# Attention then a mixture of experts on one core: the first sequence's queries taken in two passes, and the running expert begun in the 11th slot

## The chip, the cores and the metric

The kernel runs on one core of one Trainium2 chip, as one launch. The metric is the time of that launch on the device in microseconds (us), the median of 3 runs. Less is better. The core has a matmul engine (TensorE, PE in the rows; PEld is its weight load, which overlaps), a vector engine (VectorE, DVE), a scalar engine (ScalarE, ACT), a general engine (GpSimd, POOL) and a queue engine (SyncE, SP) that here issues nearly all transfers between the chip's memory and the core. Each engine runs its own instructions strictly in the order of the program and waits for others through semaphores.

## What is computed

Causal attention over 4 sequences of 576 tokens with 8 heads of 64, whose scores get a bias from a running sum; then 8 experts, all of them applied to all 2304 tokens, weighted by a normalised gate.

```python
cum = np.cumsum(np.maximum(s, 0.0), axis=-1)
bias = -(cum[:, :, :, None] - cum[:, :, None, :])
scores = np.where(causal, -1e9, q @ k.T / sqrt(D) + np.minimum(bias, 0.0))
attn = softmax(scores)
x = (attn @ v) laid out as [2304, 512]
P = exp(x @ w_gate - max); 8 rounds of row and column normalisation
out = sum over e of P[:, e] * (relu(x @ w1[e]) @ w2[e])
```

All of it is in 32-bit floats. The kernel carries each operand of a matmul as a high part and a low part (what is left after the rounding to the matmul's format), and makes three products of them.

## The kernel before

**The attention** works on head pairs: `g` counts the 16 pairs (4 sequences of 4 pairs). A pair has 5 slots, one for each block of queries `i`: four of 128 queries, and a last one that takes the 64 left of both heads together. Slot `i` needs the first `i + 1` blocks of keys. `slots` (line 662) is the list of all 80, pair after pair. The loop over `ti` (line 711) writes a pipeline: `st0` makes the scores of slot `ti` (line 497, tile `sc`), the row minimum on VectorE (line 506) and the exponential on ScalarE (line 538); `st1` the division, one slot later; `st2` the transposes (line 569, tile `tr`), two slots later; `st3` the product with v (line 599, tile `pv`), for blocks 0 and 1 together and for blocks 2, 3 and 4 together, three slots after the last of them. Its result goes into the tile `xh`, the operand of the experts.

**What a head needs** is made by `load_head` (line 329; four transfers, two halves of q and two of k, each copied to both halves of the partitions) and `prep_head` (line 408): q in two forms (`qa`, `qb`), k in two forms (`ka`, `kb`), made by GpSimd and VectorE, with two or three short transfers of bias rows and one of `qa` into `qb`, all issued from SP. `qa` and `qb` are four fixed tiles each, used by head number modulo 4 (names qa_224, qb_225 to qa_236, qb_237 in the order of before; qa_218, qb_219 to qa_230, qb_231 in that of the changed kernel). `prep_head` stands after slots 1 and 3 of the pair before.

**The running expert** is expert 0, computed beside the attention in four units of 256 hidden columns. A visit is one unit applied to the 256 to 384 tokens of one or two blocks (`EARLY`): `g1_half` (line 148) makes 6 of the 12 matmuls of a hidden block, `g2_chunk` (line 177) 6 matmuls of 512 columns. `Stream` (line 200) keeps them in a queue; `fill` (line 685) takes from it so that the queue is empty when the next sequence ends. A sequence's four visits are put into the queue in its last slots (`ti` 22, 42, 62); the fourth sequence's run after the attention. Each unit's weights come by two transfers of 512 KB (`w_load_early`, line 654, tile `wraw`) and four splits into high and low parts (lines 110 and 111, tile `w`). Two units fit; the first two are loaded and split from `ti` 4 on.

**The rest**, experts 1 to 7, runs after the attention in one long stretch of matmuls (lines 1012, 1133, 1190).

**What sets the order.** The scheduler that writes the engines' orders follows the priorities of the program and its own clock; the result is a fixed order on each engine. On SP each transfer carries one of eight semaphores in turn and waits for the transfer eight before it.

## Time and profile before

| | us |
|---|---|
| median of 3 runs | 1697.48 (1696.84 to 1698.23) |
| the profiled execution | 1700.61 |
| its span in the profile | 1698.7 |
| TensorE busy | 1667.0 (98%) |
| VectorE busy | 1192.2 (70%) |
| GpSimd busy | 871.9 (51%) |
| ScalarE busy | 838.5 (49%) |

The span runs from the first to the last instruction that the profile saw. Busy time of an engine is the time in which at least one of its instructions ran. A TensorE that is busy may run at half its clock: the granted clock, PEclk, is 1.00 at 2.4 GHz, and a mean of 0.75 over a stretch says that it spent half of it at 1.2 GHz. A line such as "L497" is a line of the kernel before; "x48" is a count of instructions.

### The profile page before, as it was taken

How to read it: one execution, taken by the hardware profiler on the slowest of the kernel's cores; microseconds unless marked ns; L12 is line 12 of the kernel's file. 1: busy time of each engine (PE TensorE's matmuls, PEld its weight loads, DVE VectorE, ACT ScalarE, POOL GpSimd, SP SyncE). 2: the span in 40 equal slices, each digit the busy share in tenths (PEclk: the TensorE clock that was granted, in tenths of full speed). 3: DMA queues.
4: the chain of work that ended last, by engine and by line, in shares of the span. 5: the costliest groups of instructions: out<-in, count | busy, mean ns of one | idle time of the engine just before them, and what ended most of it. 6: DMA issues, size and time to landing. Idle time of an engine off the chain costs nothing.

```text
span 1698.7 us, 31233 instructions
## 1 busy us (share of the span) xinstructions
PE 1667.0 (98%) x11149; PEld 1569.4 (92%) x11149; DVE 1192.2 (70%) x2309; ACT 838.5 (49%) x1820; POOL 871.9 (51%) x799
## 2 busy tenths in 40 slices
PE   7899999999999999999999999999999999999999
PEld 6788888889899999998889999999999999999999
DVE  6757666655767766776448777777777777777777
ACT  5976666633543444444235444444444544444443
POOL 6757857622654554554314455554544555554453
PEclk8989999999999999999999999999999999999999
DMA  7767666374777767865965656666697666666562
GB/s 195 222 186 215 201 195 188 98 284 156 269 260 240 262 213 232 261 226 194 338 195 175 198 176 198 189 187 189 187 316 235 210 190 188 188 186 187 176 197 88
DMA packets 204988, 352.11 MB, mean 207 GB/s; under 512 B 21089, under 2 KB 103009, under 8 KB 204801
## 3 DMA queue, kind: packets, MB, share of 16 engines
q1 hardware_dynamic: 204352, 349.19, 64.6%
q8 instruction: 89, 1.46, 0.4%
q10 hardware_dynamic: 480, 0.92, 0.2%
q14 instruction: 67, 0.54, 0.1%
HBM read 249.94 MB, written 94.81 MB: 203 GB/s over the span
## 4 chain that ended last, share of the span: by engine, by line
PE 85%; DVE 7%; DMA 2%; ACT 2%; issue 2%; POOL 1%; SPq 1%; ACTq 0%; DVEq 0%; POOLq 0%
PE c L1012 31%; PE zz L1133 13%; PE zz L1190 11%; PE y L1190 10%; PE g L148 4%; PE g L177 4%; PE sc L497 3%; DVE s L987 3%; PE pv L599 3%; PE tr L569 2%; PE c L177 1%; PE c L148 1%; DVE h L252 1%; DVE z L255 1%; DMA rawk<-kT 1%
## 5 line engine op out<-in xcount | busy, mean ns | idle before, releaser
L252 POOL TENSOR_TENSOR w2o<-r,w2o 128x512 fp32r<-128x512 f32 x189 | 274.0, 1470 | 320.9 <-ACT w2o L1170 313.3
L1012 PE MATMUL c<-xS,w1o 128*128 128x384 f32 x1344 | 270.2, 337 | 4.4 <-DVE z L255 2.8
L1190 PE MATMUL zz<-w2o,h 128*128 128x256 f32 x2016 | 273.1, 279 | 0.0
L1190 PEld LDWEIGHTS zz<-w2o,h 128*128 128x128 f32 x2016 | 263.8, 188 | 0.1
L1133 PE MATMUL zz<-w2p,h 128*128 128x512 f32 x1008 | 254.7, 391 | 0.4 <-ACT h L975 0.4
L975 ACT ACTIVATE h<-z 128x384 fp32r<-128x384 f32 x252 | 130.3, 525 | 226.6 <-DVE z L255 224.7
L976 DVE SCALAR_TENSOR_TENSOR h<-z,h 128x384 fp32r<-128x384 f32 x252 | 193.3, 775 | 65.5 <-ACT h L975 61.8
L1012 PEld LDWEIGHTS c<-xS,w1o 128*128 128x128 f32 x1344 | 226.7, 188 | 8.7 <-DVE z L255 6.9
L987 DVE SCALAR_TENSOR_TENSOR s<-z,s 128x384 f32<-128x384 f32 x224 | 189.9, 885 | 60.0 <-ACT s L1050 58.7
L1133 PEld LDWEIGHTS zz<-w2p,h 128*128 128x128 f32 x1008 | 187.1, 188 | 30.3 <-ACT h L975 0.7
L252 POOL TENSOR_TENSOR h<-s,h 128x384 fp32r<-128x384 f32 x112 | 137.7, 1236 | 128.8 <-ACT h L983 127.7
L1012 PE MATMUL c<-x,w1o 128*128 128x384 f32 x1008 | 202.1, 335 | 0.2 <-DVE z L255 0.2
L1190 PE MATMUL y<-w2o,h 128*128 128x256 f32 x1512 | 199.7, 279 | 0.0
L1190 PEld LDWEIGHTS y<-w2o,h 128*128 128x128 f32 x1512 | 193.7, 188 | 0.0
L255 DVE TENSOR_TENSOR z<-c,t 128x384 f32<-128x384 f32 x252 | 136.3, 550 | 58.1 <-PE c L1012 53.2
L1012 PEld LDWEIGHTS c<-x,w1o 128*128 128x128 f32 x1008 | 169.5, 188 | 0.4 <-DVE z L255 0.4
L1116 DVE SCALAR_TENSOR_TENSOR a<-zz,prob,a 128x256 f32<-128x256 f32 (+1 forms) x210 | 111.0, 530 | 80.9 <-PE zz L1190 50.8
L983 ACT CAST h<-s 128x384 fp32r<-128x384 f32 x224 | 112.1, 514 | 87.0 <-DVE s L987 85.8
L1012 PE MATMUL c<-xS,wp 128*128 128x384 f32 x672 | 134.5, 336 | 1.4 <-DVE z L255 1.4
L1012 PEld LDWEIGHTS c<-xS,wp 128*128 128x128 f32 x672 | 118.9, 188 | 9.6 <-DVE z L255 2.7
L1170 ACT CAST w2o<-r 128x1024 fp32r<-128x1024 f32 x98 | 102.4, 1046 | 47.8 <-PE y L1190 37.9
L252 POOL TENSOR_TENSOR wp<-s,wp 128x512 fp32r<-128x512 f32 x56 | 79.5, 1420 | 83.7 <-ACT wp L911 72.5
(149 smaller groups left out, 2738.2 us busy)
## 6 DMA issues: line engine op xcount, KB each, us to landing
w1o<-w1d SPq DMA_DIRECT2D x392, 256.0 KB
w1d<-wp SPq DMA_DIRECT2D x84, 512.0 KB
r<-wu SPq DMA_DIRECT2D x70, 512.0 KB
r<-w2d SPq DMA_DIRECT2D x56, 512.0 KB
sa<-wu SPq DMA_DIRECT2D x28, 512.0 KB
w2d<-sb SPq DMA_DIRECT2D x56, 256.0 KB
wraw<-wu SPq DMA_DIRECT2D x22, 512.0 KB
xS<-xd_S SPq DMA_DIRECT2D x12, 768.0 KB
```

The costliest lines, as they stand in the source:

```text
L148: nc.tensor.matmul(ps[:, :n], lhsT=w1[:, w, o : o + P], rhs=xcols(b, x, k, n0, n), start=(k == 0 and t == 0), stop=(k == KD - 1 and t == 2),)
L252: (eng or nc.gpsimd).tensor_tensor(out=out, in0=a, in1=b, op=ALU.subtract)
L255: (eng or nc.gpsimd).tensor_tensor(out=out, in0=a, in1=b, op=ALU.add)
L975: mark["a"] = nc.scalar.activation(t[:, 0], z, AF.Relu)
L976: mark["v"] = nc.vector.scalar_tensor_tensor(out=t[:, 1], in0=z, scalar=0.0, in1=t[:, 0].bitcast(F32), op0=ALU.max, op1=ALU.subtract,)
L983: nc.scalar.copy(t[:, 0], z)
L987: nc.vector.scalar_tensor_tensor(out=out, in0=z, scalar=0.0, in1=other, op0=ALU.max, op1=op)
L1012: mm = nc.tensor.matmul(ps, lhsT=w[:, wl, k], rhs=x[:, xl, k], start=(fresh and k == 0 and t == 0), stop=(k == 1 and t == 2), skip_group_c ...
L1116: nc.vector.scalar_tensor_tensor(out=a, in0=ps, scalar=prob[:, c, e : e + 1], in1=a, op0=ALU.mult, op1=ALU.add)
L1133: mm = nc.tensor.matmul(zb[ci], lhsT=h[:, a, ci * P : (ci + 1) * P], rhs=w[:, b_], start=(ui == 0 and f == 0 and t == 0), stop=(ui == UPE ...
L1170: nc.scalar.copy(w[:, :, 0], r)
L1190: nc.tensor.matmul(ps, lhsT=h[:, a, ci * P : (ci + 1) * P], rhs=w[:, ui, b_], start=(fresh and ui == 0 and t == 0), stop=(ui == UPE - 1 an ...
```

## The change

The first sequence (`AB = (0,)`) is taken in two passes. In pass A come slots 0 and 1 (the first 256 queries) of all four pairs, in pass B slots 2, 3 and 4 of all four; the other sequences keep their order. So the list of slots reads, for the first sequence, pair 0: 0, 1; pair 1: 0, 1; pair 2: 0, 1; pair 3: 0, 1; pair 0: 2, 3, 4; and so on. Its 256 first tokens become a block of their own for the running expert, so that there are five stages of four visits instead of four.

- Loads: for pass A two heads come in one transfer of 64 x 2 x 256 (four such for a pair); for pass B each head's other 320 queries, and all its 576 keys again. Each head of the first sequence is prepared twice, once for each pass.
- The running expert: the visits of the first 256 tokens are put into the queue at `ti` 10 (`FILLS`) and spread to slot 23, those of the next block at 22, spread to slot 33 (`UNTIL`); those of the second and third sequences at 42 and 62 as before, spread to 62 and 82. One stage more needs two units' weights more: 4 transfers of 512 KB and 8 splits.
- The weights of the first two units are loaded from `ti` 1 on, and the second unit's high parts are made on GpSimd instead of ScalarE.
- The gate's weights are split on GpSimd instead of VectorE, at `ti` 1 instead of 6.
- The first sequence's results are stored (`spill`) at `ti` 24, 27, 30 and 33 instead of within the sequence.
- Heads 2 and 3 get their bias rows from the tile `cr`, and the store of `cr` comes after them.

```diff
+AB = (0,)
...
+    stages = []
+    for b in range(B):
+        stages += [(b, [x]) for x in EARLY[b]] if b in AB else [(b, EARLY[b])]
     visits = []
-    for b in range(B):
-        order = (0, 1, 2, 3) if b % 2 == 0 else (2, 3, 0, 1)
-        visits += [(b, u, EARLY[b], oi) for oi, u in enumerate(order)]
+    for k, (b, blocks) in enumerate(stages):
+        order = (0, 1, 2, 3) if k % 2 == 0 else (2, 3, 0, 1)
+        visits += [(b, u, blocks, oi) for oi, u in enumerate(order)]
...
+    inst = []
+    for b in range(B):
+        for ph in "AB" if b in AB else "F":
+            inst += [(b * NPAIR + hp, ph) for hp in range(NPAIR)]
...
+        for i in {"A": (0, 1), "B": (2, 3, 4), "F": (0, 1, 2, 3, 4)}[ph]:
+            where[g, i] = ip
+            slots.append((g, i))
...
+        qc, kc = {
+            "A": (slice(0, 2 * P), slice(0, 2 * P)),
+            "B": (slice(2 * P, S), slice(0, S)),
+            "F": (slice(0, S), slice(0, S)),
+        }[ph]
...
-        nc.vector.tensor_copy(wg[:, :, 0:8], wgv)
-        nc.vector.tensor_tensor(
+        nc.gpsimd.tensor_copy(wg[:, :, 0:8], wgv)
+        nc.gpsimd.tensor_tensor(
...
-        nxt = min([x for x in (23, 43, 63) if x > ti] + [NS + 3])
-        budget[0] += len(stream.queue) / (2.0 * (nxt - ti))
-        while budget[0] >= 0.5:
+        left = [(e - stream.done, x) for e, x in ends if e > stream.done]
+        if left:
+            budget[0] += max(n / (2.0 * max(1, x - ti)) for n, x in left)
+        while budget[0] >= 0.5 and stream.queue:
...
+    for b in range(B):
+        FILLS += [20 * b + 10, 20 * b + 22] if b in AB else [20 * b + 22]
+        UNTIL += [20 * b + 23 + 2 * b, 20 * b + 33 + 9 * b] if b in AB else [20 * b + 42]
+    UNTIL = [min(x, NS + 3) for x in UNTIL]
...
-        if ti == 6:
+        if ti == 1:
             gate_weights()
...
+        for u in range(2):
+            r = ti - (1 + 4 * u)
+            if r in (0, 2):
...
+                w_split_early(u, r - 3, nc.gpsimd.tensor_copy if u else nc.scalar.copy)
```

**SP, the transfers from the second pair on.** In the kernel before, this is the stretch from the first weights (the 43rd transfer) to the second (the 52nd), with the preparation of head 4 and the loads of head 7:

```order
L657 DMA wraw<-wu 128x1024
L416 DMA qb_225<-crow_d 4x576
L419 DMA kb<-crow_d 4x576
L423 DMA qb_225<-qa_224 64x640
L340 DMA rawq<-qT 64x576
L341 DMA rawq<-qT 64x576
L340 DMA rawk<-kT 64x576
L341 DMA rawk<-kT 64x576
L677 DMA wgr<-w_gate 128x32
L657 DMA wraw<-wu 128x1024
```

In the changed kernel the 55th to the 69th transfer, from the second weights to the last of what pair 0 needs in pass B (tile numbers 219 and 223 are those of its two heads):

```order
L743 DMA wraw<-wu 128x1024
L567 DMA vt_234<-v 128x2x128
L498 DMA qb_219<-crow_d 4x320
L501 DMA kb<-crow_d 4x576
L506 DMA qb_219<-qa_218 64x320
L397 DMA rawq<-qT 64x320 x2
L397 DMA rawk<-kT 64x576 x2
L743 DMA wraw<-wu 128x1024
L567 DMA vt_236<-v 128x2x128
L498 DMA qb_223<-crow_d 4x256
L498 DMA qb_223<-crow_d 4x64
L501 DMA kb<-crow_d 4x576
L506 DMA qb_223<-qa_222 64x384
```

What the first pair needs for its slots 2 to 4 was in the queue's first 10 transfers before and ends with the 69th now. The last `qb<-qa` of pair 3 of the first sequence was the 77th transfer and is the 119th now, with six `wraw` transfers ahead of it instead of three.

**TensorE, the scores of pair 3 of the first sequence.** Before, they stand among transposes alone (heads 6 and 7 are tiles 232, 233, 236, 237):

```order
L569 MATMUL tr<-ident,T 128x128 x2
L497 MATMUL sc<-ka,qa_232 128x128
L497 MATMUL sc<-kb,qb_233 128x128
L569 MATMUL tr<-ident,T 128x128 x2
L497 MATMUL sc<-ka,qa_236 128x128
L569 MATMUL tr<-ident,T 128x128 x3
L497 MATMUL sc<-ka,qa_232 128x256
L497 MATMUL sc<-kb,qb_233 128x256
L497 MATMUL sc<-kb,qb_237 128x128
```

In the changed kernel the scores of the same heads' later queries (tiles 226, 227, 230, 231), in pass B:

```order
L152 MATMUL g<-xh,w_1013 128x256 x2
L181 MATMUL g<-w_781,hh 128x512 x2
L181 MATMUL g<-w_781,hl 128x512
L181 MATMUL g<-w_781,hh 128x512 x2
L181 MATMUL g<-w_781,hl 128x512
L652 MATMUL tr<-ident,T 128x128 x6
L580 MATMUL sc<-kb,qb_227 128x384
L580 MATMUL sc<-kb,qb_227 128x512
L152 MATMUL g<-xh,w_1013 128x256 x6
L580 MATMUL sc<-kb,qb_231 128x384
L181 MATMUL g<-w_781,hh 128x512 x2
```

Visits of the running expert (lines 152 and 181) now stand between them, and behind `sc<-kb,qb_231` in the queue.

**TensorE, at pair 3 of the second sequence.** Its first product with v (`pv<-at`, 6 matmuls; `vt` is the tile of v) stands beside the scores of the third sequence's first pair, around slots 40 to 42. Before:

```order
L599 MATMUL pv<-at,vt_242 64x128 x6
L569 MATMUL tr<-ident,T 128x128 x5
L177 MATMUL g<-w_1926,hh 128x512 x2
L177 MATMUL g<-w_1926,hl 128x512
L569 MATMUL tr<-ident,T 128x128 x2
L497 MATMUL sc<-ka,qa_224 128x384
L497 MATMUL sc<-kb,qb_225 128x384
L148 MATMUL g<-xh,w_2147 128x256 x12
L569 MATMUL tr<-ident,T 128x128 x4
L497 MATMUL sc<-ka,qa_228 128x384
L497 MATMUL sc<-kb,qb_229 128x384
```

And in the changed kernel:

```order
L580 MATMUL sc<-ka,qa_222 128x256
L580 MATMUL sc<-kb,qb_223 128x256
L683 MATMUL pv<-at,vt_236 64x128 x6
L652 MATMUL tr<-ident,T 128x128 x3
L580 MATMUL sc<-ka,qa_218 128x384
L580 MATMUL sc<-kb,qb_219 128x384
L652 MATMUL tr<-ident,T 128x128 x4
L580 MATMUL sc<-ka,qa_222 128x384
L580 MATMUL sc<-kb,qb_223 128x384
```

The visits that stood here are gone: those of the first sequence have been spread to slot 33, and the next are put into the queue at slot 42.

## Rows read from the trace of the kernel before

**Rows 1.** The page: busy time of each engine, share of the span, instructions.

```profile
PE 1667.0 (98%) x11149; PEld 1569.4 (92%) x11149; DVE 1192.2 (70%) x2309; ACT 838.5 (49%) x1820; POOL 871.9 (51%) x799
```

**Rows 2.** Stretches of 10 us: length, each engine's busy us, granted clock, DMA share.

```profile
0.00:10.00 10.00, 7.01 (x42) 6.57 (x42) 6.48 (x8) 3.39 (x5) 7.83 (x27) 1.00 0.61 145
10.00:20.00 10.00, 8.65 (x32) 7.01 (x32) 7.22 (x29) 7.95 (x27) 4.67 (x6) 0.66 0.83 217
20.00:30.00 10.00, 7.76 (x83) 6.61 (x83) 5.30 (x14) 3.69 (x9) 7.25 (x10) 0.83 0.74 201
30.00:40.00 10.00, 5.92 (x30) 4.21 (x29) 7.13 (x28) 7.12 (x24) 6.94 (x9) 0.93 0.77 202
40.00:50.00 10.00, 9.25 (x55) 7.42 (x54) 7.36 (x25) 8.95 (x27) 9.57 (x9) 0.73 0.75 211
50.00:60.00 10.00, 7.71 (x90) 6.37 (x88) 8.17 (x30) 8.69 (x24) 6.29 (x7) 0.96 0.85 249
60.00:70.00 10.00, 9.90 (x94) 8.70 (x93) 6.65 (x25) 9.39 (x29) 7.44 (x9) 0.87 0.68 175
70.00:80.00 10.00, 8.62 (x64) 6.51 (x64) 9.01 (x34) 9.56 (x32) 7.25 (x8) 1.00 0.82 228
80.00:90.00 10.00, 7.03 (x79) 6.65 (x75) 6.46 (x26) 9.06 (x27) 9.70 (x10) 0.82 0.73 204
90.00:100.00 10.00, 9.94 (x57) 8.34 (x56) 3.76 (x12) 4.93 (x17) 3.59 (x4) 0.67 0.71 195
```

**Rows 3.** The chain that ended last, in order of time: start us, us, what.

```profile
13.23 3.08 DMA rawk<-kT
...
80.61 6.63 DMA qb<-qa
...
101.99 2.26 PE pv L599 x48
...
119.63 1.42 PE g L148 x12
...
125.67 1.39 PE g L177 x6
...
189.14 2.26 PE pv L599 x48
```

**Rows 4.** SP's own time line, transfers being issued: start us, us, what.

```profile
13.88 0.59 SPq L487 DMA_DIRECT2D vt<-v  x1
...
30.02 0.59 SPq L657 DMA_DIRECT2D wraw<-wu  x1
...
37.00 0.37 SPq L677 DMA_DIRECT2D wgr<-w_gate  x1
...
45.20 0.49 SPq L423 DMA_DIRECT2D qb<-qa  x1
...
52.55 0.52 SPq L423 DMA_DIRECT2D qb<-qa  x1
...
80.61 0.51 SPq L423 DMA_DIRECT2D qb<-qa  x1
...
96.48 0.52 SPq L423 DMA_DIRECT2D qb<-qa  x1
```

**Rows 5.** TensorE's time line: a wait for a transfer in the attention's head.

```profile
87.38 0.77 PE L497 MATMUL sc<-kb,qb 68*128 68x128 f32 x2 [2.98 <-DMA qb<-qa]
```

**Rows 6.** ScalarE's time line: the last exponentials of the fourth and the fifth pair.

```profile
71.04 0.78 ACT L538 ACTIVATE T<-T,mn 128x576 f32<-128x576 f32 x1 [0.44 <-DVE mn L506]
...
82.73 0.78 ACT L538 ACTIVATE T<-T,mn 128x576 f32<-128x576 f32 x1 [0.50 <-DVE mn L506]
```

**Rows 7.** Groups by line and shape from 0 to 100 us: busy us, mean ns.

```profile
L111 POOL TENSOR_TENSOR w<-wraw,w 128x512 fp32r<-128x512 f32 x12 | 15.2, 1276 | 4.0 <-ACT w L110 3.7
...
L110 ACT CAST w<-wraw 128x512 fp32r<-128x512 f32 x12 | 6.8, 613 | 3.5 <-DMA wraw<-wu 3.5
...
L347 PE MATMUL g<-ones 128*128 128x128 f32 x40 | 6.4, 336 | 1.0 <-POOL ones L344 1.0
```

More of the change, by code (lines that the diff above doesn't have):

```diff
@@ L203, in __init__ @@
             self.queue = []
+            self.done = 0
         def add_visit(self, vi, load, split):
@@ L227, in add_visit @@
                     seq += g1[:2] + late[:2] + g1[2:3] + late[2:] + g1[3:]
-            if vi + 1 in loads:
+            if len(blocks) == 1:
+                hooks = {}
+                if vi + 1 in loads and vi:
+                    for pc, x in enumerate((0, 1, len(seq) - 2, len(seq) - 1)):
+                        hooks.setdefault(x, []).append(
+                            lambda pc=pc: split(loads[vi + 1], pc)
+                        )
+                if vi + 2 in loads:
+                    for pc, x in enumerate((2, len(seq) - 1)):
+                        hooks.setdefault(x, []).append(
+                            lambda pc=pc: load(loads[vi + 2], (pc,))
+                        )
+                for x, fs in hooks.items():
+                    seq[x] = (lambda fs=fs, f0=seq[x]: ([f() for f in fs], f0()))
+            elif vi + 1 in loads:
                 nu = loads[vi + 1]
@@ new lines, in spans, with prep_head @@
+    def spans(n):
+        h, ph, _, o = spot(n)
+        if ph == "A":
+            return (0, o, 2 * P), [(0, o, 2 * P)]
+        lo = 2 * P if ph == "B" else 0
+        at = [(lo, lo, S - lo)] if h % 2 == 0 else [(lo, lo, S - D - lo), (S - D, S, D)]
+        return (0, 0, S), at
+    def prep_head(n):
+        h, ph, r, off = spot(n)
+        rq, rk = raws.pop((n, "q")), raws.pop((n, "k"))
+        ka, kb = keys(n)
+        qa, qb = qas[r], qbs[r]
+        rows = crow_d[h : h + 1] if n > 3 else cr[h : h + 1].bitcast(F32)
+        (ki, ko, kn), at = spans(n)
+        kc, rc = slice(ko, ko + kn), slice(ki, ki + kn)
+        for i, o, w in at:
@@ L529, in st0 @@
                 for jj in range(2):
-                    scores(sc[:, :288], 2 * g + jj, 4, cols, jj == 0, jj == 1)
+                    scores(sc[:, :288], 2 * where[t] + jj, 4, cols, jj == 0, jj == 1)
                 row_min(
@@ L660, in w_split_early @@
         split_piece(u, pc, wraw[pc // 2][:, pc % 2 * 512 : (pc % 2 + 1) * 512], hi)
-    slots = [(g, i) for g in range(B * NPAIR) for i in range(5)]
     NS = len(slots)
-    NG = B * NPAIR
     da = first_heads()
     with tc.issue_after(da.ins):
+        load_unit(1)
+    with tc.issue_after(heads_in[0].ins):
+        rows_in = [prep_head(n) for n in (2, 3)][-1]
+    with tc.issue_after(rows_in.ins):
         nc.sync.dma_start(out=crow_d, in_=cr.bitcast(F32))
-        load_head(2)
+        load_unit(2)
         load_v(0)
-        load_head(3)
+        load_unit(3)
+        load_v(1)
+    PREP = {}
+    for ip, (g, ph) in enumerate(inst[2:], 2):
+        f, q = min(x for x in range(NS) if where[slots[x]] == ip), g % NPAIR
+        if f < 8:
+            a = ((0, 1), (2, 3))[q - 2]
+        elif ph == "A":
+            a = (f - 4, f - 3)
+        else:
+            a = (f - 3 if ph == "B" and q == 0 else f - 4, f - 2)
+        for j in range(2):
+            PREP.setdefault(a[j], []).append(2 * ip + j)
+    for a in PREP.values():
+        a.sort()
     wgr = const.tile([P, KD * 8], F32, name="wgr")
@@ L712, in fused_kernel @@
         if ti < NS:
-            g, i = slots[ti]
-            if i == 4 and g + 1 < NG:
-                load_v(g + 1)
             for j in heads(slots[ti]):
@@ L1210, in step2 @@
                 store_out(c)
-    for vi in range(12, 16):
+    for vi in range(len(visits) - 4, len(visits)):
         stream.add_visit(vi, w_load_early, w_split_early)
```

212 lines of the change are left out of this document (125 added, 87 removed).

## The prediction

> **What bounds the kernel now.** The page comes first: TensorE is busy for 1667.0 of 1698.7 us [rows 1]. The other engines have room on average, so the time is TensorE's work plus what TensorE loses, and a change that leaves its work alone can only move the loss. Both orders hold the same matmuls, so I ask one question: how much does TensorE lose before, where, and how much after?
>
> The stretches of 10 us tell where [rows 2]. From 0 to 100 us TensorE is busy 7.01 + 8.65 + 7.76 + 5.92 + 9.25 + 7.71 + 9.90 + 8.62 + 7.03 + 9.94 = 81.8 us, so 18.2 us are idle; the whole span has 31.7. The granted clock falls below 1 in eight of the ten stretches; the missing parts add up to 0.34 + 0.17 + 0.07 + 0.27 + 0.04 + 0.13 + 0.18 + 0.33 = 1.53 stretches, 15.3 us. And 6.4 us of the busy time are warm-up matmuls on ones [rows 7]. Together some 40 us of the first 100 do nothing for the result. That is the pool from which the change can draw: it brings work of the running expert into slots in which TensorE has too little to do.
>
> Behind 100 us TensorE is the bound, and there its work can be priced. From the close of one pair to the close of the pair four later, 101.99 to 189.14, are 87.2 us [rows 3]. In them the running expert takes 512 tokens: 4 units x 2 blocks x (2 x 1.42 for 12 matmuls each + 2 x 1.39 for 6 wide ones) [rows 3] = 45.0 us. That leaves 42.2 us of attention, 10.5 us for a pair. Counted by columns and transposes, blocks 0 and 1 (pass A) are a quarter of a pair, 2.5 us, and blocks 2 to 4 (pass B) the rest, 8.0 us (estimates).
>
> Now what loses the 40 us. The attention's head is paced by SP's queue. A transfer holds it 0.59 us even where it is a small one [rows 4]; the last transfer that a head needs is the 65th at 45.20, the 77th at 52.55, the 120th at 80.61 and the 140th at 96.48 [rows 4], which is 0.68 us for each one from the 65th to the 140th. The difference to 0.59 is waiting: the 43rd transfer, 512 KB of weights, is issued at 30.02, and the one eight behind it can go only at 37.00 [rows 4]. What comes behind weights lands late: 6.63 us from issue to landing at 80.61 against 3.08 early on [rows 3]. TensorE then stands for 2.98 us [rows 5] and afterwards gets a clock of 0.67 [rows 2]. On the other hand the engines are not slow when the data are there: the fifth pair's last exponential comes 11.7 us after the fourth's [rows 6].
>
> **The change part by part.** *The running expert comes earlier.* Pass A's blocks are complete by slot 8, and 22.5 us of visits (half of 45.0) move from slots 22 to 42 into slots 10 to 23. If every one of them fell into lost time, the gain would be 22.5 us; that is the ceiling.
>
> *SP's queue is longer ahead of it.* Each head of the first sequence is prepared twice. By the order, the second head of pair 0 has what its pass B needs with the 69th transfer, and pair 3's with the 119th, where the old order had served pair 3 with the 77th. Weights ahead of the 119th: six transfers of 512 KB, and the old order has as many ahead of its 120th, so the old times hold for the new places. The 69th: 45.20 + 4 x (52.55 - 45.20) / 12 = 47.7 us. The 119th: 80 us.
>
> *Point one, the 69th.* A second load of weights stands five places ahead of it, so I take a landing between 3.08 and 6.63 us, nearer to the short one: the scores of head 1 can go on at 51 us (50.8 to 54.3). Behind them in TensorE's order stand all further visits. What TensorE has done by then: four times pass A (10.0), the first scores of pass B, ten matmuls of the running expert (1.2) and half the gate, 12.4 us in all. Lost: 51 - 12.4 = 38.6 us, nearly as much as the kernel before loses until 100.
>
> *Point two, the 119th.* From 51 us TensorE has enough to do. Up to the last scores of pair 3 the order puts pass A (10.0), pass B of pairs 0 to 2 with parts of pairs 2 and 3 (20), 10.8 us of visits and 1 of gate: 41.8 us, so TensorE would be there at 51 + 29.4 = 80.4. The transfer is issued at 80 and lands at 83 to 87; two loads of weights stand ahead of it, as they did at 80.61 [rows 3]. TensorE waits 3 to 6 us, with half a stage of visits queued behind those scores, which nobody can take out of their order. I take 3.5: lost 42.1. Behind that the transfers lead again: the 138th goes out at some 95 us, TensorE needs it at 42 + 57.4 = 99.5.
>
> *The clock.* The wait between pass A and 51 us is longer than the one of 2.98 us. Between nothing and 3.3 us (the 0.33 of the stretch from 90 to 100) are lost again while TensorE has dense work; I take 1.
>
> *The hole.* The visits of the second block end at slot 33 and the next come at 42, so for two pairs there is attention alone. TensorE's work there is 2 x 10.5 = 21 us with some gate, and the pace of the other engines without visits is 11.7 us [rows 6], 23.4. Lost between 0 and 2.4 us, and as much at slot 20, where one stage has run out and the next has just begun; I take 1.5 for both.
>
> *The splits.* Two units more: 8 x 0.613 = 4.9 us on ScalarE and 8 x 1.276 = 10.2 us on GpSimd [rows 7], four high parts more on GpSimd, about 2.5 us. GpSimd is busy for 70.5 of the first 100 us [rows 2], so the 12.7 us and the second preparation of eight heads have 29.5 us of room beside TensorE's work, and I cost them at nothing. Without that cover a visit waits for its weights; two splits in a row, 2.5 us, is the price I hold for that. The gate's split leaves VectorE, where it is off the path from then on: nothing. The stores of the first sequence leave the head; that is in the count of transfers. From slot 42 on both orders have the same visits with the same slots: nothing.
>
> *The sum.* After: 42.1 + 1 + 1.5 = 44.6 us lost. Before: 40. The change loses 4 us more (rounded down). The profiled execution would go from 1700.61 to some 1704.6, and it lay 3.1 above the median; the median goes from 1697.5 to 1701.5.
>
> **The rivals.** *The queue keeps up* (faster). All rests on when the 69th and the 119th transfer land. Without waits for weights the 69th goes out at 30.02 + 17 x 0.59 + 9 short ones of bias rows at 0.37 = 43.4 us [rows 4] and lands 3.08 later, at 46.5; the second wait disappears and the clock stays up. Lost: 46.5 - 12.4 + 1.5 = 35.6, a gain of 4.4 us, 1693; with the hole at nothing as well, and the two splits' 2.5 us taken out of the waits that the kernel before had, it ends at 1689. It decides at a landing of the 69th before 47.5 us. For it: pass A's transfers are smaller, and three of the loads of weights come late in the stretch. Against it: the wait of the transfer eight places behind the weights, from 33 to 37.00 us [rows 4], stands in the new order too.
>
> *It cancels* (no change). The clock and the hole cost nothing and the wait at point two is 1 to 2 us: lost 40, 1697.5, give or take 3.4. For it: every term of the sum is a few us, and the two losses of 40 differ by less than their errors.
>
> *The bytes set the pace* (faster). Transfers then follow their sizes: up to the 119th some 12.7 MB by the shapes in the order, at 203 GB/s (mean of [rows 2]) 62 us instead of 80. Pass B would be ready as soon as ScalarE has ended pass A, at about 41 us; lost 41 - 12.4 + 1.5 = 30, gain 10, 1687.5. Against it: 0.59 us for a transfer whatever its size [rows 4]. The Trainium skill has this as a rule (DMA: Bandwidth & Descriptors, section Issuing engines are not separate DMA queues): the time to start a transfer on an engine is usually small beside the transfer. By that rule the result is this rival's; the 0.59 us here is a fifth of the 3.08 us, and with a new transfer behind each it is not small.
>
> **How the numbers follow.** About 0.2%, 3.4 us, is what a measurement of this kernel can tell from no change. Forecast (slower, 1699 to 1709, with the second wait at its 6 us, the clock at 3.3 and the splits uncovered at the upper end: 4 + 2.5 + 2.3 + 2.5 = 11): 0.42. It cancels (1694 to 1701): 0.28. The queue keeps up (1689 to 1694): 0.22. The bytes: 0.08. Faster 0.30, same 0.28, slower 0.42. The range from 1688 to 1709 leaves out the bytes' case and the upper tail, under 2 in 10; the likeliest case's own range is 1699 to 1709.
>
> **What would show it.** In the changed kernel: the 69th and 119th transfers of SP's time line near 48 and 80 us; TensorE idle until about 51 us in scores (line 580) that wait for `qb<-qa`, and again for 3 to 6 us at 80 to 87; a granted clock under 1 up to 60 us and close to 1 from there; the close of pair 3's pass B near 107 us (the old order's fifth pair closed at 101.99); TensorE a little idle between slots 33 and 42, some 125 to 175 us. The step is wrong if pass B starts before 46 us, if TensorE's order stalls on weights of the running expert (lines 111 and 112) instead of on heads, or if the hole costs more than 5 us, which would be seen as a pace of over 13 us for a pair there.

## The result and the profile after

The changed kernel takes 1712.72 us (median of 6 runs, 1711.52 to 1714.51) where the kernel before takes 1697.12 us in the same set: 15.6 us longer, a ratio of 1.0093 (95% interval 1.0080 to 1.0106). The forecast was slower by 4 us, with a range to 1709. The direction was right, the size was not. The profiled execution's span grew by 13.0 us, from 1698.7 to 1711.7.

TensorE's work is the same, as expected: 11149 matmuls before [rows 1] and after. The page of the changed kernel, busy time of each engine:

```profile
PE 1671.5 (98%) x11149; PEld 1572.7 (92%) x11149; DVE 1194.7 (70%) x2315; ACT 839.4 (49%) x1819; POOL 890.5 (52%) x834
```

Stretches of 10 us of the changed kernel, TensorE alone: length, busy us, granted clock, DMA share, GB/s (before: [rows 2]):

```profile
0.00:10.00 10.00, 8.11 (x45) 1.00 0.30 75
10.00:20.00 10.00, 4.43 (x17) 0.67 0.56 138
20.00:30.00 10.00, 7.17 (x38) 0.50 0.54 143
30.00:40.00 10.00, 5.26 (x19) 0.50 0.59 170
40.00:50.00 10.00, 8.65 (x38) 0.50 0.81 228
50.00:60.00 10.00, 8.80 (x42) 0.50 0.58 163
60.00:70.00 10.00, 10.00 (x66) 0.95 0.56 153
70.00:80.00 10.00, 9.25 (x97) 1.00 0.76 222
...
130.00:140.00 10.00, 9.11 (x73) 1.00 0.80 238
150.00:160.00 10.00, 8.89 (x66) 1.00 0.91 278
160.00:170.00 10.00, 9.24 (x101) 1.00 0.73 204
170.00:180.00 10.00, 5.54 (x27) 0.69 0.68 212
```

From 10 to 60 us TensorE does little and does it at or near half clock. From 60 to 120 it is nearly dense at full clock. Between 130 and 180 it is short of work again, which the kernel before never is between 100 and 320 us. To put that into one number for each part, I count a stretch as **lost** by 10 us minus busy time times granted clock, and add up:

| lost, us | 0 to 60 | 60 to 110 | 110 to 200 | sum |
|---|---|---|---|---|
| before | 21.2 | 10.3 | 0.0 | 31.5 |
| after | 34.0 | 1.6 | 9.9 | 45.4 |
| difference | +12.8 | -8.8 | +9.9 | +13.9 |

The sum agrees with the 13.0 us of the spans; from 200 to 400 us both lose the same, 1.9 and 1.8. So there are two losses: a net 4.0 us up to 110 us (12.8 - 8.8), and 9.9 us in a part that the prediction priced at 1.5. Of the 9.9, 2.6 lie before 160 us, where visits still stand in the order, and 7.2 from there on, in the hole.

The measure has an error of its own. The run "x sums late" below has the same order on TensorE up to 188 us; by the measure it loses 4.0 us less up to 110 us, yet it closes pair 3 only 1.0 us earlier. So a difference in the head is good to some 3 us, and the net 4.0 are hardly clear of that.

**Where the 9.9 us go.** TensorE's time line of the changed kernel (start us, us, what, in brackets the idle time before it and what ended it), and VectorE's at the same place:

```profile
168.72 0.51 PE L652 MATMUL tr<-ident,T 128*128 128x128 f32 x3
174.46 0.58 PE L580 MATMUL sc<-ka,qa 128*128 128x256 f32 x1 [5.22 <-DVE mn L589]
```

```profile
169.19 0.16 DVE L640 RECIPROCAL rec<-sm 128x2 f32<-128x2 f32 x1
173.06 0.91 DVE L504 CAST ka<-rawk 128x576 fp32r<-128x576 f32 x1 [3.72 <-POOL sc L275]
173.89 0.51 DVE L589 CUSTOM_DVE_ANT_0 T<-sc,mask,mn 128x288 f32<-128x288 f32 x1
```

TensorE waits 5.22 us for a row minimum. VectorE could make that minimum at once, but in its queue the cast of the keys of a later head (`ka`, line 504) stands first, and the cast waits. That cast reads the raw keys, whose second half SP issues at 170.01 us. (The profile names a sum on GpSimd that ends at 173.06; the cast doesn't read it, and a landing just before that moment would look the same.) Behind the wait the clock falls to 0.69. VectorE's waits from 110 to 200 us in the changed kernel, by what it did next and what it waited for: us in total, times, longest:

```profile
DVE ka L504 <- DMA rawk<-kT: 5.0, 2, 3.1
DVE ka L504 <- POOL sc L275: 3.7, 1, 3.7
...
DVE ka L504 <- POOL qa L503: 1.4, 2, 1.2
```

The three rows are 10.1 us in front of this one cast; only the first is put down to raw keys by the profile. In the same view of the kernel before the cast has no line at all.

**The head.** TensorE's waits from 8 to 200 us in the changed kernel, the same columns:

```profile
PE tr L652 <- ACT T L643: 9.1, 7, 2.2
PE sc L580 <- DVE mn L589: 6.1, 2, 5.2
PE g L152 <- ACT w L111: 3.2, 1, 3.2
...
PE sc L580 <- DMA qb<-qa: 0.2, 1, 0.2
```

Nearly all of the first and all of the third line lie before 60 us: it waits for ScalarE's divisions (`tr` for `T`), which come behind VectorE's row minima, and 3.2 us for the running expert's first weights. It hardly waits for `qb<-qa`.

### The profile page after: what moved, and what is told of

Read it like the earlier page. It is cut to its first block, busy times and chain, and to the rows that moved or that the text cites. A ratio compares the mean times of both kernels' runs of the same rounds, so it can differ in the third digit from the quotient of the medians.

```text
span 1711.7 us, 31370 instructions
## 1 busy us (share of the span) xinstructions
PE 1671.5 (98%) x11149; PEld 1572.7 (92%) x11149; DVE 1194.7 (70%) x2315; ACT 839.4 (49%) x1819; POOL 890.5 (52%) x834
## 4 chain that ended last, share of the span: by engine, by line
PE 83%; DVE 6%; DMA 3%; POOL 2%; issue 2%; ACT 2%; SPq 1%; ACTq 0%; DVEq 0%; POOLq 0%
PE c L1127 31%; PE zz L1248 13%; PE zz L1305 11%; PE y L1305 10%; PE g L152 4%; PE g L181 4%; PE sc L580 3%; DVE s L1102 2%; PE pv L683 2%; PE tr L652 2%; PE c L181 1%; PE c L152 1%; DVE h L272 1%; DMA w1o<-w1d 1%; DVE z L275 1%
```

## The experiments

A load unit is what the changed kernel loads at once: units 0 to 3 are the pairs of pass A, 4 to 11 the heads of pass B, from 12 on the heads of the later sequences. Each time stands against the kernel before in the same set of runs, since its median moves between 1695.3 and 1697.4 from set to set; the changed kernel is 15.6 us above it. The lost times are those of one execution each. Against the changed kernel, "visits to slot 42", "both", "TensorE kept busy" and "10 loads on ScalarE" differ by no more than the noise: their intervals of the ratio overlap its 1.0080 to 1.0106.

An edit that moves or adds transfers also made the scheduler write another order on the other engines, so it doesn't change the queue alone. TensorE's order differs from 13.0 us on with 20 loads on ScalarE and from 19.4 us on with 16 transfers more. It stays as it was up to 86 us with look-ahead 3, up to 127 us with visits to slot 42, and up to 188 us with the x sums late.

| kernel | median, us | above before | lost 0 to 60 | 60 to 110 | 110 to 200 |
|---|---|---|---|---|---|
| after | 1712.7 | 15.6 | 34.0 | 1.6 | 9.9 |
| look-ahead 3 | 1709.1 | 11.8 | 31.2 | 3.3 | 3.0 |
| visits to slot 42 | 1710.4 | 13.1 | 32.7 | 1.2 | 7.5 |
| both | 1711.3 | 13.9 | 34.1 | 3.0 | 6.1 |
| visits late | 1727.8 | 30.5 | 33.2 | 13.3 | 6.1 |
| cast on GpSimd | 1729.3 | 34.0 | 29.8 | 10.0 | 13.9 |
| TensorE kept busy | 1713.7 | 18.4 | 17.4 | 4.4 | 7.2 |
| 20 loads on ScalarE | 1700.9 | 5.6 | 24.7 | 2.9 | 2.8 |
| one load for two | 1952.5 | 257.2 | 41.6 | 29.1 | 50.9 |
| 20 loads, look-ahead 3 | 1707.4 | 11.0 | 23.2 | 6.6 | 3.8 |
| 12 loads, look-ahead 3 | 1701.5 | 5.1 | 27.2 | 2.3 | 2.8 |
| x sums late | 1706.5 | 9.4 | 29.0 | 2.6 | 2.9 |
| weights on ScalarE | 1718.4 | 21.2 | 32.8 | 3.2 | 11.8 |
| 20 loads, x sums late | 1698.4 | 1.2 | 22.8 | 2.9 | 1.6 |
| 10 loads on ScalarE | 1711.3 | 14.2 | 31.7 | 2.5 | 7.8 |
| 20 loads spread | 1703.4 | 6.0 | 24.5 | 2.9 | 2.1 |
| 16 loads spread | 1699.7 | 2.3 | 25.0 | 2.0 | 1.6 |
| before, 16 loads on ScalarE | 1701.8 | 5.4 | 25.6 | 10.1 | 0.0 |
| before, 16 transfers more | 1703.9 | 7.5 | 23.2 | 11.9 | 0.0 |

### The late stretch: look-ahead or hole

**Look-ahead 3.**

```diff
-    nrx = max(u for u in range(u0 + 2) if u % 5 == 0) + 1
+    nrx = 21
```

> Edit: the extra staging for raw queries and keys (rx, three heads) is kept until the head that the old order gave it up with (nrx 21 where the change computes 11), so from the 11th load unit to the 21st a head's raw data are asked for three heads ahead and not two; the sums of the first x block, which take over that memory, start behind 17 more transfers. Nothing else moves. Theory A (starved preparation): the 5.2 us in which TensorE stands at 169 us, and the lower clock behind it (3.4 us in the stretches from 170 to 190), come from raw keys asked for too late. Then both go, and most of the 3.4 us of idle time between 130 and 170: 1701 to 1705. Theory B (the hole): without visits from slot 33 to 42 TensorE goes at the pace of the other engines whatever the raw data do; the same time as the changed kernel, 1711 to 1714, with the idle time only moved. Theory C (the head): the loss is the half clock of the first 60 us; no change either, 1711 to 1714.

The loss between 110 and 200 us falls from 9.9 to 3.0, as theory A has it; the wait of 5.2 us is gone, and VectorE's waits in front of `ka` fall from 10.1 to 2.4 us. In the hole (pair 7, without visits) the pair closes 12.2 us after the one before. But the time falls by 3.8 us only and ends above the range of A. The span fell by 5.8.

**Visits to slot 42**, and **both**.

```diff
-    UNTIL += [20 * b + 23 + 2 * b, 20 * b + 33 + 9 * b] if b in AB ...
+    UNTIL += [20 * b + 23 + 2 * b, 20 * b + 42] if b in AB ...
```

> Edit: the second block of the first sequence is spread until slot 42 and not until 33, so that visits stand in all slots up to where the next stage begins; nothing else. Theory B (the hole): visits fill the waits of 130 to 175 us, and 7 to 11 us come back, 1702 to 1706. Theory A (starved preparation): the head whose raw keys come late is needed in the same place of the order, but TensorE reaches it later by the visits that now stand ahead of it, about half of the block's last ten slots; a part comes back, 3 to 6 us, 1707 to 1710. Theory C (half clock in the first 60 us): nothing, 1711 to 1714.

> Edit: both, the staging kept (nrx 21) and the block spread until slot 42. Theory A: no more than the staging alone, 1701 to 1705. Theory B: no more than the spread alone. If the two losses are separate, the gains add, 1695 to 1700. What then still lies above the kernel before (1697) is what the head of the program costs.

2.5 us come back with the hole filled, and 1.7 us with both, neither clear of the noise; both edits together end above every forecast for them but theory B's. Theory B falls: with visits in every slot VectorE still stands 8.0 us waiting for raw keys, and 7.5 us are still lost; only the place moves, to 180 to 190 us. The gains don't add either, so neither setting alone is "the" cause of the 15.6.

**Visits late.**

```diff
-    FILLS += [20 * b + 10, 20 * b + 22] if b in AB ...
+    FILLS += [20 * b + 21, 20 * b + 22] if b in AB ...
-    UNTIL += [20 * b + 23 + 2 * b, 20 * b + 33 + 9 * b] if b in AB ...
+    UNTIL += [20 * b + 33, 20 * b + 42] if b in AB ...
```

> Edit: the first sequence keeps its two passes, but both blocks of the running expert wait until slots 21 and 22 and are spread until slots 33 and 42, about where the old order had them; so only the order of the heads and the side edits are left of the change. By the prediction's account the early visits sit in time that TensorE loses otherwise: pass A alone leaves it even emptier, and the 11 us of visits that stood between 60 and 110 us now come on top, 1715 to 1725. Theory A or B (the loss lies at 130 to 175 us, not at the head): the waits there are filled by the visits, so 1700 to 1706 in spite of an emptier head. Theory C (half clock in the first 60 us): the clock there is as low or lower, with 1.2 us less work at it; 1711 to 1716.

14.9 us slower than the changed kernel, above even the 1715 to 1725 of the prediction's account. The loss from 60 to 110 us grows by 11.7, the 11 us of visits that I had counted there. This way of counting, work against lost time, holds here: the two passes with the side edits cost some 30 us, and the early visits give half of that back.

### Who is blocked, and does the clock cost

**Cast on GpSimd.**

```diff
-        nc.vector.tensor_copy(ka[:, kc], rk[:, rc])
+        nc.gpsimd.tensor_copy(ka[:, kc], rk[:, rc])
```

> Edit: in the preparation of a head (line 504) the cast of the keys goes to GpSimd and not to VectorE; nothing else. In the changed kernel VectorE stands 10.1 us between 110 and 200 us in front of this cast, because the raw keys have not landed, and the row minima behind it, for which TensorE waits, stand too; in the kernel before it does not stand there at all. Theory A (the cast that blocks VectorE is what costs): TensorE's wait of 5.2 us at 169 us goes, and so do VectorE's waits in front of this cast in pass A (5.9 us between 12 and 26 us): 1702 to 1707. Rival (late keys are late whoever casts them): the wait turns into one of TensorE's scores for a head, and GpSimd has 0.7 us more per head: 1711 to 1716.

18 us slower than the changed kernel, outside both ranges. That VectorE is blocked is not disproved, but this remedy is worse: TensorE's waits for `T` grow from 9.1 to 14.2 us, and pass B starts with a loss of 10.0 us from 60 to 110. That it is because the preparation of a head now runs in one line on GpSimd was not tried. (The expectation's 5.9 us in pass A are 3.9 in the trace.)

**TensorE kept busy.**

```diff
                 st2(slots[ti - 2], j)
+                for _ in range(4 if ti < 10 else 0):
+                    nc.tensor.matmul(idle[:, :P], lhsT=ident, rhs=T[:, :P], ...)
```

> Edit: behind the transposes of each tile of pass A stand four matmuls more (128x128 of the tile T with the identity, into a bank that nobody reads), 64 in all; everything else as in the changed kernel. They only keep TensorE busy while it waits for the other engines. Theory C (the half clock of the first 60 us is a loss of its own, 16.4 us): the granted clock in the five stretches from 10 to 60 us rises from 0.5 to 0.8 or more, and the visits and pass B from 38 to 60 us go at full speed; the time falls by 4 to 9 us, 1704 to 1709. Theory D (the transfers on SP's queue and the engines behind them pace the first 60 us, and the clock only fills the waits): the clock rises and the idle time with it, and the time is the same or a little longer by the matmuls that stand in front of others, 1711 to 1717.

The granted clock from 10 to 60 us, stretches as above:

```profile
10.00:20.00 10.00, 7.50 (x49) 0.83 0.55 139
20.00:30.00 10.00, 7.12 (x55) 0.83 0.56 154
30.00:40.00 10.00, 8.69 (x70) 1.00 0.60 170
40.00:50.00 10.00, 8.45 (x65) 1.00 0.71 211
50.00:60.00 10.00, 8.23 (x45) 0.68 0.60 169
```

The clock rises from 0.50 to 0.83 and 1.00, and the time is 2.8 us longer, which the noise covers. The added matmuls (128 in the trace) are busy for 19.2 us; taken out of the 16.6 us of apparent gain (34.0 to 17.4), nothing is left. Theory C's gain of 4 to 9 us did not come, and theory D's range holds. That the half clock costs nothing doesn't follow: the added matmuls stand in TensorE's queue, and what they cost there was not separated from what the clock gave back. Two pairs of kernels with the same order say more (last section).

### SP's queue

**20 loads on ScalarE.**

```diff
-    eng = nc.scalar if u == 0 and which == "k" else nc.sync
+    eng = nc.scalar if (u == 0 and which == "k") or 1 <= u < 6 else nc.sync
```

> Edit: the raw queries and keys of load units 1 to 5 (pairs 1 to 3 of pass A and pair 0 of pass B, 20 transfers) are issued by ScalarE and not by SP; nothing else. Theory D (SP's queue paces the head: it issues without a pause from 8 to 60 us, some 0.6 us a transfer, and VectorE, ScalarE and TensorE wait for raw keys and for weights): 20 transfers less put everything behind them up to 12 us earlier, the first weights at 22 us and not at 32.7; of the 34 us lost in the first 60 a third goes, 1700 to 1705. Theory C (the clock): pass A stays a chain of small steps with a half clock, a gain of 0 to 3 us, 1709 to 1713. Against both: if an issue holds ScalarE as long as it holds SP, 12 us of issues stand in front of its exponentials, 1712 to 1722.

10.0 us of the 15.6 come back (ratio to before 1.0031, 1.0021 to 1.0040), as theory D forecast. By the lost times of the two single executions, which add up to more, 9.2 us come back in the first 60 us, and with them 7.0 of the 9.9 in the late stretch, whose transfers the edit doesn't touch. All of VectorE's waits in front of `ka` there fall from 10.3 to 5.7 us. That the late keys hang on the same queue as the head fits this; shown is only that both losses fall together. ScalarE pays for it; its time line (ACTq is its transfer queue):

```profile
18.36 0.60 ACTq L397 DMA_DIRECT2D rx<-qT  x1
...
25.56 1.31 ACTq L397 DMA_DIRECT2D rx<-kT  x2
26.97 0.51 ACT L621 ACTIVATE T<-T,mn 128x256 f32<-128x256 f32 x1 [7.60 <-DMA rx<-qT]
```

Twelve issues, 0.49 to 0.81 us each, stand in one piece in front of an exponential, whose row minimum VectorE had ended at 19.0 us.

**One load for two.**

```diff
-    for t in range(2):
-        eng.dma_start(out=raw[t * D : (t + 1) * D, ...], in_=src[h, :, cs])
+    nc.sync.dma_start(out=raw[:, ...],
+                      in_=src[h, :, cs].unsqueeze(0).to_broadcast([2, D, n]))
```

> Edit: from load unit 4 on (pass B and all later sequences) the raw queries of a head come with one transfer of 128 partitions that reads the 64 rows twice, and not with two of 64 partitions, and so do the keys; the data and bytes are the same, SP issues 2 transfers less for each head, 18 less ahead of the 119th. Theory D (SP's queue): the first weights go out 2.4 us earlier, pass B's last head 8 to 10 us earlier, and raw keys in the stretch from 110 to 200 us land in time; the loss there (9.9 us) goes to 3 or less and 2 to 4 us of the head come back, 1700 to 1706. Rival (the bytes or the chain of buffers set when raw data land, not the number of transfers): the same time, 1710 to 1714.

240 us slower. The chain of waits shows why: one such transfer takes 19 to 21 us to land; in the changed kernel's chain a half of the keys takes 2.7 to 4.0.

```profile
409.43 19.48 DMA rawk<-kT
```

So this says nothing about the number of transfers: in this form (one transfer, its source with a leading dimension of 2 that repeats the 64 rows) the transfer itself is slow.

**20 loads with look-ahead 3**, and **12 loads with look-ahead 3**.

```diff
-    nrx = max(u for u in range(u0 + 2) if u % 5 == 0) + 1
+    nrx = 21
-    eng = nc.scalar if u == 0 and which == "k" else nc.sync
+    eng = nc.scalar if (u == 0 and which == "k") or 1 <= u < 6 else nc.sync  # or u < 4
```

> Edit: the raw data of load units 1 to 5 issued by ScalarE (20 transfers off SP's queue), and the staging for a third head ahead kept (nrx 21), both as tried alone; nothing else. Theory D (one cause: raw data are asked for too late, in the head because SP's queue is full, later because they are asked for only two heads ahead): of the 2.8 us that the first edit alone still loses between 110 and 200 us the second takes away 1 to 3, 1697 to 1700, level with the kernel before. Rival (the shorter queue has already healed the later stretch): nothing, 1700 to 1702.

> Edit: as the run before this one, but only load units 1 to 3 (the rest of pass A, 12 transfers) go to ScalarE, so that 8 issues of 0.65 us less stand in front of ScalarE's exponentials between 18 and 27 us, and SP gets these 8 back. Theory D: SP is what is short, so 5 us of SP's time come back into the head and 2 to 4 us are lost against it: 1700 to 1704. Rival (ScalarE's issues are by now what holds up pass A: it stood 7.6 us there): 1693 to 1697.

With 20 loads the look-ahead makes it worse by 5.4 us (11.0 above before and not 5.6), outside both forecasts: 6.6 us are lost from 60 to 110. With 12 loads it is level with the 20 loads alone. That lies in theory D's range, but not for its reason: fewer loads off SP were to cost 2 to 4 us against the run before, and are 5.9 us better. A longer look-ahead asks for more raw data while the head still needs SP; that this is the reason was not tried.

**The kernel before, 16 loads on ScalarE**, and **16 transfers more**.

```diff
-    eng = nc.scalar if h < 2 and which == "k" else nc.sync
+    eng = nc.scalar if (h < 2 and which == "k") or 2 <= h < 6 else nc.sync
```

> Edit on the kernel before, not on the changed one: the raw data of heads 2 to 5 (16 transfers) issued by ScalarE and not by SP. Theory D: SP's queue is the pace of this head too (0.68 us for a transfer from the 65th to the 140th), but it has 42 transfers less ahead of pair 3's last head; a gain of 3 to 8 us, 1688 to 1693, smaller than the 12 us that the changed kernel gained. Rival (only the longer queue of the changed order is a bound): no gain, 1695 to 1699, or a loss by ScalarE's issues, up to 1703.

```diff
     heads_in[0] = eng.dma_start(out=raw[D:], in_=src[h])
+    for x in range(2 if 2 <= h < 6 else 0):
+        nc.sync.dma_start(out=scr[:, i], in_=src[h, 0:4, 0:64])
```

> Edit on the kernel before: beside the raw data of heads 2 to 5 SP issues 16 small transfers more (4 rows of 64 from DRAM to DRAM, read by nobody), 1 KB each; nothing else. This measures what a transfer more in SP's queue costs by itself. Theory D: 0.3 to 0.6 us each, 5 to 10 us in all, and nearly all of it is seen in the time: 1701 to 1706. Rival (SP has slack in the old order, or the waits behind weights hide it): 1696 to 1699.

The old order doesn't gain from ScalarE's help; it loses 5.4 us. That is against theory D, which forecast a gain of 3 to 8, and in the range of its rival (a loss by ScalarE's issues, up to 1703). Sixteen transfers more cost it 7.5 us (ratio 1.0047, 1.0032 to 1.0062), 0.47 us each. SP's time line of that kernel, shortest, median and longest issue in ns:

```profile
L345 SPq DMA_DIRECT2D scr<-qT x8: 579/600/701, 4.4 to 29.8; - x8
```

Each holds SP 0.60 us though it moves 1 KB, and what the sixteen cost in time is four fifths of that. TensorE's waits for `qb<-qa` up to 110 us come to 7.4 us, where the kernel before has the 2.98 us of [rows 5]. This speaks for theory D, since 16 KB at the some 200 GB/s of [rows 2] are 0.1 us (an estimate). It is no clean test, since the order of the other engines changed with it. The Trainium skill (DMA: Bandwidth & Descriptors, section Issuing engines are not separate DMA queues) calls the time to start a transfer usually small beside the transfer; here the starts of sixteen transfers take 9.6 us of SP's queue, which is not small.

**10 loads on ScalarE** and **weights on ScalarE.**

```diff
-    eng = nc.scalar if u == 0 and which == "k" else nc.sync
+    eng = nc.scalar if which == "k" and u < 6 else nc.sync
```

> Edit: of load units 1 to 5 only the raw keys (10 transfers) on ScalarE's queue, the raw queries stay on SP's. Theory D with a price for ScalarE's issues (0.65 us each, 7.6 us in one piece when it was 20): half of both, 1700 to 1704. Rival (SP's queue alone counts): half of the gain of 12 us, 1705 to 1708. Rival (ScalarE's issues had eaten a part of the gain): more than the gain of 12 us, 1695 to 1700.

```diff
-    w_load_early(u, (r // 2,))
+    w_load_early(u, (r // 2,), nc.scalar)
```

> Edit: on the changed kernel, the four loads of weights of the first two units (512 KB each) are issued by ScalarE at its start and not by SP between 32 and 56 us; nothing else. Theory D (SP's queue is what is short in the head): four transfers less and none of the waits behind them, 4 to 7 us of SP's time; TensorE's wait of 3.2 us for weights at 38 us goes as well: 1704 to 1708. Rival (one MB of weights at the start delays the first heads, and ScalarE waits for free buffers): 1711 to 1718.

Half the loads give 1.4 us and not half of the gain, outside all three forecasts. The raw queries stay in SP's queue, and a head needs both; whether that is the reason was not tried. The first weights on ScalarE's queue, from the start, cost 5.6 us, where theory D forecast a gain: TensorE is idle for 22 of the first 60 us, and for 18 in the changed kernel. So theory D, right for the 20 loads and for the 16 transfers more, is wrong for these two and for the old order's 16 loads: not every relief of SP pays.

### The x sums

**x sums late**, and **20 loads with x sums late**.

```diff
+    qd[n] = (the last transfer of prep_head(n))
     for i, o in enumerate(XRAW):
-        nc.sync.dma_start(out=xs[a][:, i], in_=xd[p, o][:, :, k, ts])
+        with tc.issue_after(qd[27].ins):
+            nc.sync.dma_start(out=xs[a][:, i], in_=xd[p, o][:, :, k, ts])
```

> Edit: on the changed kernel, the loads for the sums of the first x block (sx<-xd) are put behind the preparation of the pair 9 (the tenth); they otherwise begin two pairs earlier, at 148 us, and their sums stand on GpSimd between the preparations of the heads, and their loads on SP between the raw loads. Theory E (the sums hold up the preparation that frees the raw buffers): the raw keys that came late at 173 us come in time, the loss between 110 and 200 us falls from 9.9 to 4 or less, and the time to 1704 to 1708. Rival (the look-ahead of two heads is what is short, and the kernel before had these sums in the same place without a wait): no change, 1711 to 1714.

> Edit: the raw data of load units 1 to 5 on ScalarE's queue (20 transfers off SP) and the x sums behind the preparation of pair 9. Theory E with D: the 2.8 us that were left between 110 and 200 us go as well, 1697 to 1699. Rival: 1700 to 1703.

Alone it brings 6.2 us (1706.5); the late stretch loses 2.9 and not 9.9. No wait of VectorE in front of `ka` there is put down to raw keys any more (4.4 us to other things). This is the cleanest test of the late stretch, since TensorE's order is the same. TensorE begins the closing products of pairs 6 and 7, and SP the last raw keys that pair 7 waits for, in the changed kernel:

```profile
164.94 0.80 PE L683 MATMUL pv<-al,vt 128*64 128x64 f32 x20
183.95 0.80 PE L683 MATMUL pv<-al,vt 128*64 128x64 f32 x20
170.01 0.59 SPq L397 DMA_DIRECT2D rawk<-kT  x1
```

and with the x sums late:

```profile
163.08 0.80 PE L686 MATMUL pv<-al,vt 128*64 128x64 f32 x20
175.63 0.80 PE L686 MATMUL pv<-al,vt 128*64 128x64 f32 x20
160.95 2.12 SPq L398 DMA_DIRECT2D rawk<-kT  x2
```

The keys go out some 8 us earlier, and a lead of 1.9 us becomes one of 8.3. Theory E holds beside theory A: the raw keys come in time when they are asked for earlier, and also when GpSimd and SP have no sums between the preparations. With the 20 loads the changed order comes to 1698.37 us, 1.2 above the kernel before (ratio 1.0013, 1.0004 to 1.0022).

### What is left

**20 loads spread**, and **16 loads spread** (both with x sums late).

```diff
+    if ti < 4 and j == 1:
+        load_unit(2 + ti)      # behind the exponential of slot ti; second kernel: u < 5
```

> Edit: as the run with units 1 to 5 on ScalarE's queue and the late x sums, but the loads of units 2 to 5 are asked for one unit a slot, behind the exponentials of slots 0 to 3, so that the 12 issues that stood in one piece in front of ScalarE's exponentials (18 to 27 us) come in pieces of 8 and 4. Theory F (ScalarE's issues hold up pass A by now): 1 to 3 us back, 1695 to 1697. Rival (the raw data then come later, and SP and ScalarE lose alike): the same, 1697 to 1700.

> Edit: as the run before this one, with unit 5 back on SP's queue (4 transfers); one piece of 8 issues on ScalarE is left. Theory F: 2.6 us of issues less on ScalarE, 2.4 us more on SP; better than the run before it by 1 to 2 us, 1693 to 1696, which would beat the kernel before. Theory D (SP alone counts): worse by 2 us, 1698 to 1701.

Spread, the 20 loads lose 4.8 us against the same loads in one piece; with 16 the time is 2.3 above before. Neither theory forecast the first. The second lies in theory D's range, but theory D had it worse than the first, and it is 3.7 us better, the way theory F pointed. None of these kernels beats the kernel before. What holds up the rest of the head stays open.

## Why the prediction was wrong

**Right: the two points in SP's queue.** The 69th and the 119th transfer were forecast at 47.7 and 80 us (before: [rows 4]). SP's time line of the changed kernel:

```profile
47.05 0.49 SPq L506 DMA_DIRECT2D qb<-qa  x1
...
78.58 0.49 SPq L506 DMA_DIRECT2D qb<-qa  x1
```

**Near in sum, by luck, and wrong in its parts: the head.** Up to the end of pass B the forecast was 42.1 + 1 - 40 = 3.1 us more loss than before; measured up to 110 us are 4.0, good to some 3. The sum hides two errors. The 40 of before is 2 us too high: its 15.3 us of clock count idle time that stands in the 18.2 already; of busy time the clock took 13.3. And the steps were other ones. The wait until 51 us was to be one for `qb<-qa` at line 580; that wait is 0.2 us in all. TensorE stood for `T` and for the first weights, and went at half clock. Its first scores of pass B, those of head 1, and the split that the weights held up:

```profile
41.88 1.48 PE L580 MATMUL sc<-ka,qa 128*128 128x384 f32 x3
...
53.56 0.95 PE L580 MATMUL sc<-kb,qb 68*128 68x384 f32 x2
```

```profile
37.57 1.14 ACT L111 CAST w<-wraw 128x512 fp32r<-128x512 f32 x2 [3.25 <-DMA wraw<-wu]
```

So pass B started before 46 us, and head 1 went on at 53.6 us without waiting for its transfer. Both that and a stall on weights had been named as signs against the step. The stall was 3.2 us; it ended with ScalarE's split, which itself had waited 3.25 us for the transfer, so it was the transfer that was late and not the splits that lacked cover. **Point two**, 3.5 us, did not occur, and the second half of that stretch went better than forecast. **The clock**, 1 us, was 3.6 by the measure: what the lower clock takes of the busy time up to 110 us adds up to 16.9 after against 13.3 before. How much of that is time is not known. The close of pair 3's pass B, forecast near 107 us, begins at 108.28 in the chain of waits (before, the fifth pair closed at 101.99 [rows 3]):

```profile
108.28 2.26 PE pv L683 x48
```

**The step that failed: "The hole", 1.5 us.** The late stretch cost 9.9, 7.2 of them in the hole itself. I priced it by the pace of the other engines, 11.7 us for a pair [rows 6]. That pace was right: with the look-ahead restored the pair in the hole closes in 12.2 us. What I left out is whether the raw data are there at that pace. They were not, and they are late at a slower pace too: with visits to slot 42, VectorE still stood 8.0 us for raw keys. The price's own test, a pace of over 13 us for a pair, came true: 19.0 us from the close of pair 6 to that of pair 7, 5.2 of them the one wait. Two things that the diff and the trace did show make the keys late, and neither had a line in the sum. One is `nrx`: the staging that holds a third head ahead ends at load unit 10 in the changed kernel, where the old one kept it to head 16. The other is the x sums on GpSimd and SP, which before begin at 130 us, also behind the close of pair 5, without harm. Undoing either takes 6.9 and 7.0 us off the late stretch, and 3.8 and 6.2 us off the time. "From slot 42 on: nothing" was right: from 200 to 350 us neither kernel loses anything.

**The rest.** 8.4 us for the late stretch and 0.9 for the head make 13.3 out of the forecast 4, beside the 13.0 of the spans. The other 2.6 us of the 15.6 are the two profiled executions, of which that of before lay 3.1 us above its median.

**The rivals.** "The queue keeps up" needed the 69th transfer to land before 47.5 us; it was issued at 47.05 and held SP until 47.54. "The bytes set the pace" needed the 119th at some 62 us; it went out at 78.58. "It cancels" needed a hole at no cost. Shown is that late raw keys block VectorE and through it TensorE in the late stretch, and that an earlier request or the x sums out of the way undo most of it. That SP's queue carries much of the rest is likely (10.0 us come back with 20 loads off it, 7.5 us are lost with 16 transfers more), but not shown alone: the orders changed with both edits, and three other reliefs of SP went against theory D. Open stay what holds up the head otherwise, the last 1 to 2 us, and why the longer look-ahead, good for 3.8 us alone, costs 5.4 together with the 20 loads.

## What to carry to other kernels

Where transfers are small and many, count them in the issuing queue ahead of the work that needs them; here that count gave the queue's times to 1.5 us, and the bytes did not. Moving them to another engine costs time in that engine's queue. When an edit makes a stretch faster, ask what must be there earlier for it, and price the look-ahead of every buffer that feeds it. An instruction that waits for a transfer in the middle of an engine's queue stops all that is behind it: look for such waits on the engines between the queue and the one that is short, and put the transfer earlier or other work out of its way.

## What the runs showed of the hardware

- An issue holds SP 0.60 us at 1 KB (median), and ScalarE 0.49 to 0.81 us at 80 to 144 KB. It is time on that engine's own queue: ScalarE did nothing for 7.60 us behind twelve of them.
- One transfer of 288 KB whose source repeats 64 rows by a leading dimension of 2 took 19.5 to 21 us; as two transfers of 64 rows each takes 2.7 to 4.0.
- The clock differs between kernels whose instructions are the same, and what it costs depends on the waits behind. The changed kernel and the one with late x sums have the same order on every engine up to the x sums, near 148 us, yet from 50 to 60 us one ran at 0.50 and the other at 0.92. The same 12 matmuls and the next wide ones in the changed kernel, and then with the x sums late (with the row of the clock):

```profile
57.81 2.76 PE L152 MATMUL g<-xh,w 128*128 128x256 f32 x12
63.14 0.63 PE L181 MATMUL g<-w,hh 128*128 128x512 f32 x2
```

```profile
50.00:60.00 10.00, 8.53 (x59) 0.92 0.70 194
55.31 1.58 PE L152 MATMUL g<-xh,w 128*128 128x256 f32 x12
58.23 0.50 PE L583 MATMUL sc<-ka,qa 128*128 128x512 f32 x1 [0.93 <-DVE mn L592]
62.04 0.74 PE L181 MATMUL g<-w,hh 128*128 128x512 f32 x2 [1.53 <-DVE hl L163]
```

A lead of 1.0 us at 51 us (a product with v begins at 51.15 and 50.16) becomes 2.5, and two waits take it back to 1.1: there the half clock cost nothing that lasted. The kernels with 20 loads on ScalarE, without and with the x sums late, have the same order on TensorE up to 167 us. Both begin the same score at 36.61 us; from 38 to 40 us the first has a clock of 0.50 and the second of 1.00:

```profile
36.61 0.66 PE L580 MATMUL sc<-kb,qb 68*128 68x384 f32 x1 [1.48 <-DMA qb<-qa]
43.08 0.88 PE L683 MATMUL pv<-at,vt 128*64 128x128 f32 x12
```

```profile
36.61 0.42 PE L583 MATMUL sc<-kb,qb 68*128 68x384 f32 x1 [1.16 <-DMA qb<-qa]
40.61 0.88 PE L686 MATMUL pv<-at,vt 128*64 128x128 f32 x12
```

Here 2.5 us are gained by the next product with v, and the close of pair 5 is still 2.5 us earlier (142.94 and 140.49 us). A profiled head of a single execution differs by that much for the same order, so the medians decide.
